# Sinkhorn attention with a mixture of experts: later queries interleaved by ScalarE, keys mixed two rows at a time

## The chip, the core and the metric

One core of a Trainium2 chip. The metric is the device time of one execution in microseconds (us). The first comparison of the kernel before with the changed kernel has four runs of each. A ratio is always the mean of one kernel's fast runs over the mean of the fast runs of before from the same rounds. That is why it is not quite the ratio of the medians that are quoted beside it. A run is "fast" when it lies within 1.5% of the fastest run of the same kernel; all runs that are compared were fast, or "unknown" where there was only one.

## The reference

Block attention: in each of 32 (batch, head) pairs the 768 rows fall into 8 blocks of 96. A Sinkhorn matrix P, from five rounds of row and column normalization, mixes the blocks of keys and values; each block of queries then attends to one mixed block. A mixture of four experts follows.

```python
k_sorted = np.einsum('bhij,bhjcd->bhicd', P, k_b)        # v the same way
scores = scale * np.matmul(q_b, k_sb.transpose(0, 1, 2, 4, 3))   # per block
attn = softmax(scores)
x = matmul(attn, v_sb)            # [4, 8, 768, 64] -> rows of 512
for e in range(4):
    out += p[:, e:e+1] * (np.maximum(x @ w1[e], 0) @ w2[e])
```

## The kernel before

Batch 0's attention is the "head" of the program (to about 45 us). While TensorE works on one batch's experts, the attention of the next batch runs in slots between groups of matmuls, by a fixed plan. In this program the matmuls write their results to PSUM and read their operands from SBUF. `psA` and `psM` are two pools of PSUM with two buffers each; keys, values, scores and averages of the attention share `psA`.

```python
PLAN = [(0, 0, st_q, 0), (0, 1, st_v, 0), ..., (0, 6, st_s, 0), ..., (0, 9, st_a, 0), ...]  # (chunk, slot, stage, pair of heads)

def load_queries(b, heads=range(H)):            # one DMA a head, rows of 64 floats
    ...
    for h in heads:
        nc.gpsimd.dma_start(t[:, h // 2, :, h % 2, :], q[b, h].rearrange("(t p) d -> p t d", p=P))

def st_q(b, pr):                                # queries of two heads, transposed by the DMA
    nc.sync.dma_start_transpose(qT[:], natural[(b, "q")][:, pr].rearrange("p t h d -> p (t h d)"))

def st_k(b, pr):                                # keys: mixed and transposed in one matmul
    for r in range(R):                          # R = 6
        for hh in range(2):
            nc.tensor.matmul(ps[ds(D * hh, D), r, :], head(b, "k", h)[:, r, :], PIk..., ...)
    nc.scalar.copy(kT..., ps...)                # one copy, 128x768

def st_s(b, pr):                                # scores, then the exponential
    for i in range(NB):
        for hh in range(2):
            nc.tensor.matmul(pss[hh]..., kT[...], qT[ds(D * hh, D), i, :], ...)
    for hh in range(2):
        nc.scalar.activation(ETs[...][:, 0:S].rearrange("c (a x) -> c a x", a=2), pss[hh][0:BLK, :, 0:HS], AF.Exp, ...)
```

The softmax here doesn't subtract the row's maximum and nothing guards it: scores larger than these inputs give would overflow.

## Time and profile before

| | before |
|---|---|
| time, median of 4 | 374.87 us (374.79 to 375.55) |
| span of the profiled run | 373.0 us |
| TensorE busy | 366.3 us |
| ScalarE busy | 73.9 us |
| exponential of a score group | 24 x 0.802 us |

TensorE's own waits are the measure here: it is busy nearly all the time, so a change helps only by giving it less to do or by removing an idle stretch, and hurts by making one. The prediction shows these lines.

### The profile page before, as it was taken

To read this page: it belongs to the slowest core of one execution; us is meant where nothing else is said; L and a number is where in the kernel's file an instruction comes from. 1 tells how busy PE (TensorE), PEld (TensorE's weight loads), DVE (VectorE), ACT (ScalarE), POOL (GpSimd) and SP (SyncE) were. 2 spreads that over 40 slices of the span, in tenths; PEclk is the share of its full clock that TensorE was granted. 3 is DMA by queue.
4 is the path that set the end of the run, shared out by engine and by line. 5 is a ranking of instruction groups with operands and counts; after the bars stand their busy time and mean duration, and the time that the engine had idled before them with its cause. 6 is when DMAs were issued, how large, how long until landed. Compare 5 with 4: busy or idle time off the path is not lost.

```text
span 373.0 us, 9188 instructions
## 1 busy us (share of the span) xinstructions
PE 366.3 (98%) x4013; PEld 314.9 (84%) x4013; DVE 261.2 (70%) x470; ACT 73.9 (20%) x120; POOL 87.9 (24%) x122
## 2 busy tenths in 40 slices
PE   8999999999999999999999999999999999999996
PEld 8785858888888888888898888888889888888885
DVE  5654798679888774795694684696695693774872
ACT  2673330423210233012100224012101000000000
POOL 8772101804577203002911000000000001001001
PEclk9999999999999999999999999999999999999999
DMA  7999999999995658642962322505203101121001
GB/s 104 207 207 229 208 209 197 190 163 143 187 154 137 110 77 133 126 80 43 124 71 48 101 66 60 138 2 77 79 2 79 57 15 44 56 47 50 19 3 56
DMA packets 69603, 38.25 MB, mean 103 GB/s; under 512 B 40374, under 2 KB 64444, under 8 KB 69564
## 3 DMA queue, kind: packets, MB, share of 16 engines
q0 software_dynamic: 34640, 17.83, 37.6%
q1 hardware_dynamic: 34924, 19.85, 26.0%
q8 instruction: 31, 0.51, 0.6%
q14 instruction: 8, 0.07, 0.1%
HBM read 42.00 MB, written 6.34 MB: 130 GB/s over the span
## 4 chain that ended last, share of the span: by engine, by line
PE 87%; DMA 8%; DVE 2%; POOL 1%; issue 1%; ACT 0%; DVEq 0%
PE ps_h L730 40%; PE ps_p L763 35%; DMA w<-in_moe_w_dram 4%; PE ps_o L670 3%; DMA qT<-natq 2%; PE ps_w L241 2%; DMA natq<-in_q_dram 2%; PE ps_h L635 1%; PE ps_s L393 1%; PE ps_a L425 1%; PE ps_k L376 1%; PE ps_v L345 1%; POOL sn L284 0%; DVE xsl L410 0%; POOL T L136 0%
## 5 line engine op out<-in xcount | busy, mean ns | idle before, releaser
L730 PE MATMUL ps_h<-xT,w 128*128 128x256 f16 x1440 | 163.0, 273 | 0.0
L730 PEld LDWEIGHTS <-w 128*128 128x128 f16 x1440 | 139.5, 98 | 17.8
L736 DVE SCALAR_TENSOR_TENSOR Hb<-ps_h,pb 128x1024 f16<-128x1024 f32 x90 | 110.1, 1224 | 40.1 <-PE ps_h L730 38.3
L763 PEld LDWEIGHTS <-Sb 128*128 128x128 f16 x720 | 69.5, 98 | 9.6 <-issue 0.5
L763 PEld LDWEIGHTS <-Hb 128*128 128x128 f16 x540 | 52.1, 98 | 6.8 <-issue 0.4
L790 POOL TENSOR_TENSOR oa<-u,p 128x256 f32<-128x256 f32 x9 | 6.5, 723 | 176.7 <-issue 161.9
L763 PE MATMUL ps_p<-w,Sb 128*128 128x256 f16 x360 | 43.2, 273 | 0.3 <-DVE u L863 0.3
L763 PE MATMUL ps_p<-w,Hb 128*128 128x256 f16 x360 | 43.2, 273 | 0.0
L763 PE MATMUL ps_p<-T,Sb 128*128 128x256 f16 x360 | 42.3, 273 | 0.0
L400 ACT ACTIVATE ET<-ps_s 96x768 f16<-96x768 f32 x24 | 18.1, 802 | 54.4 <-PE ps_s L393 54.4
L114 POOL DMA_DIRECT2D natq<-in_q_dram x24 | 19.9, 851 | 14.3 <-DMA w<-in_moe_w_dram 10.2
L778 ACT COPY p<-ps_p 128x256 f32<-128x256 f32 x9 | 3.4, 373 | 93.3 <-PE ps_p L763 50.1
L763 PE MATMUL ps_p<-T,Hb 128*128 128x256 f16 x180 | 21.6, 273 | 0.0
L715 DVE TENSOR_TENSOR Sb<-Sb,Hb 128x512 f16<-128x512 f16 x45 | 19.6, 436 | 0.4
L717 DVE TENSOR_TENSOR Sb<-Hb 128x512 f16<-128x512 f16 x45 | 18.8, 418 | 0.0
L713 DVE TENSOR_TENSOR Sb<-Hb 128x512 f16<-128x512 f16 x45 | 18.8, 417 | 0.0
L410 DVE TENSOR_TENSOR xsl<-ps_a,rz 96x512 f16<-96x512 f32 x24 | 16.5, 686 | 0.8
L719 DVE TENSOR_TENSOR Sb<-Hb,Sb 128x512 f16<-128x512 f16 x45 | 16.6, 427 | 0.0
L383 ACT CAST kT<-ps_k 128x768 f16<-128x768 f32 x12 | 9.6, 799 | 35.4 <-PE ps_k L376 35.3
L788 DVE TENSOR_TENSOR u<-ps_p,p 128x256 f32<-128x256 f32 x9 | 3.8, 426 | 17.9 <-PE ps_p L763 17.9
L351 ACT CAST vo<-ps_v 128x768 f16<-128x768 f32 x12 | 9.5, 801 | 21.5 <-PE ps_v L345 19.8
L103 POOL DMA_DIRECT2D nat_k<-in_k_dram x8 | 6.1, 767 | 31.9 <-PE ps_k L376 27.8
(131 smaller groups left out, 300.9 us busy)
## 6 DMA issues: line engine op xcount, KB each, us to landing
w<-in_moe_w_dram POOLq DMA_DIRECT2D x7, 1024.0 KB, 27.1
pb<-p_dram SPq DMA_DIRECT2D x12, 512.0 KB, 5.1
nat_k<-in_k_dram POOLq DMA_DIRECT2D x8, 384.0 KB, 7.4
nat_v<-in_v_dram POOLq DMA_DIRECT2D x8, 384.0 KB, 8.6
vs<-vo SPq DMA_DIRECT2D x36, 66.0 KB, 4.6
natq<-in_q_dram POOLq DMA_DIRECT2D x24, 96.0 KB, 4.5
out_dram<-ob SPq DMA_DIRECT2D x9, 256.0 KB, 2.3
out_dram<-oa SPq DMA_DIRECT2D x9, 256.0 KB, 2.3
```

The lines of the kernel that those rows point to most:

```text
L114: nc.gpsimd.dma_start(t[:, h // 2, :, h % 2, :], q[b, h].rearrange("(t p) d -> p t d", p=P))
L383: nc.scalar.copy(kT[:, 0:S].rearrange("p (i r c) -> p i r c", i=NB, r=R), ps.rearrange("p r (i c) -> p i r c", c=CP),)
L400: nc.scalar.activation(ETs[2 * (pr % 2) + hh][:, 0:S].rearrange("c (a x) -> c a x", a=2), pss[hh][0:BLK, :, 0:HS], AF.Exp, bias=0.0, scale ...
L410: nc.vector.tensor_tensor(xsl[:, :, hh, :].rearrange("c (a i) d -> c a i d", a=2), av[:, :, :, 0:D], rz[:].broadcast_to([BLK, 2, HB, D]), ...
L670: nc.tensor.matmul(ps, h0(fc)[:, ds(t * P, P)], w2sb[0][:, fc, :], start=(fc == 0), stop=(fc == NFC - 1),)
L713: tt(sm[0], blk(0, 1), blk(1, 1), ALU.add)
L715: tt(sm[1], sm[0], blk(0, 0), ALU.subtract)
L717: tt(sm[2], blk(0, 0), blk(0, 1), ALU.subtract)
L719: tt(sm[3], blk(1, 0), sm[1], ALU.subtract)
L730: nc.tensor.matmul(ps[:, f, :], w1sb[e][:, kc, ds((4 * g + f) * P, P)], xT[:, kc, ds(2 * c * P, 2 * P)], start=(kc == 0), stop=(kc == NKC ...
L736: nc.vector.scalar_tensor_tensor(out=Hb[:, e, ds(4 * g, 4), :], in0=ps[:], scalar=0.0, op0=ALU.max, in1=pb[:, ds(e, 1), :].broadcast_to([P ...
L763: nc.tensor.matmul(ps[:], lhs(e, f), Ts[e][rhs][:, f, :], start=(e == es[0] and f == 0), stop=(e == E - 1 and f == KH - 1),)
```

## The change

The intent: queries are loaded in large contiguous pieces as keys are, which saves many small packets, and keys need half as many matmuls, each at full width. The price is paid on ScalarE, which is idle four fifths of the time: a copy that interleaves the queries, four key copies for one, and an exponential that writes its columns back in the old order.

```diff
 def st_q(b, pr):
-    nc.sync.dma_start_transpose(qT[:], natural[(b, "q")][:, pr].rearrange("p t h d -> p (t h d)"))
+    nc.scalar.copy(qi.rearrange("p (r h d) -> p h r d", r=R, h=2), natural[(b, "q", pr // 2)][:, ds(2 * (pr % 2), 2), :, :])
+    nc.sync.dma_start_transpose(qT[:], qi)
 def st_k(b, pr):
-    ... 12 matmuls of 64 columns of weights; one copy of 128x768
+    for hh in range(2):
+        for a in range(R // 2):
+            nc.tensor.matmul(pk[:, hh, a, :], head(b, "k", h)[:, ds(2 * a, 2), :].rearrange("p r d -> p (r d)"), PIk..., ...)
+    ... four copies of 64x384
 def st_s(b, pr):
-                qT[ds(D * hh, D), i, :],
+                qT[ds(D * hh, D), :, ds(i * CP, CP)],
 ...
-            ETs[...][:, 0:S].rearrange("c (a x) -> c a x", a=2),
-            pss[hh][0:BLK, :, 0:HS],
+            ETs[...][:, 0:S].rearrange("k (a i c r) -> k a i r c", a=2, i=HB, r=R),
+            pss[hh][0:BLK, :, 0:HS].rearrange("k a (i r c) -> k a i r c", i=HB, r=R),
 # head: the query transposes of both halves move behind the fifth exponential; 30 filler matmuls
#       (their results are not used, they keep TensorE busy) for 20 + 12
 # first batch of experts: p1 in psA instead of psM; p6 read out before a weight sum; PLAN0 reordered
 # end: the last output is stored in two halves
```

More of the change, by code (lines that the diff above doesn't have):

```diff
@@ L99, in load_natural @@
     def load_natural(b, nm, qd):
-        src = {"k": k, "v": v}[nm]
+        src = {"q": q, "k": k, "v": v}[nm]
         t = nat.tile([P, 4, R, D], F16, name=f"nat_{nm}_{b}_{qd}", tag=f"nat_{nm}")
@@ L106, in load_natural @@
         )
-    def load_queries(b, heads=range(H)):
-        if (b, "q") not in natural:
-            natural[(b, "q")] = nat.tile([P, NPB, R, 2, D], F16, name=f"natq_{b}", tag="natq", bufs=1)
-        t = natural[(b, "q")]
-        for h in heads:
-            nc.gpsimd.dma_start(t[:, h // 2, :, h % 2, :], q[b, h].rearrange("(t p) d -> p t d", p=P))
     def head(b, nm, h):
@@ L237, in warm @@
     def warm(n):
-        ps = psA.tile([P, 4, P], F32, tag="ps", name=f"ps_w_{state['n']}")
+        ps = psM.tile([P, 4, P], F32, tag="ps", name=f"ps_w_{state['n']}")
         state["n"] += 1
@@ L259 @@
     scol = const.tile([GH, NB, 1], F32, name="scol")
-    sn16 = const.tile([GH, NB, NB, CP], F16, name="sn16")
+    sn16_q = const.tile([P, NB * NB * CP], F16, name="sn16_q")
+    sn16 = sn16_q[0:GH].rearrange("g (i j c) -> g i j c", i=NB, j=NB)
+    qi = sn16_q[:, 0:2 * R * D]
     warm(84)
@@ L265 @@
         nc.scalar.activation(sn[:], sn[:], AF.Exp, bias=0.0, scale=1.0)
-        if it >= 3:
-            h_q(it - 3, 0, nc.scalar.copy)
-            warm(20 - 8 * (it - 3))
+        if it == 4:
+            for qd in range(2):
+                h_q(qd, 0, nc.scalar.copy)
+            warm(30)
         nc.vector.tensor_reduce(srow[:], sn[:], AX.X, ALU.add)
@@ L365, in st_q @@
         qT = att.tile([P, R, P], F16, name=f"qT_{b}_{pr}", tag="qT", bufs=3)
-        nc.sync.dma_start_transpose(
-            qT[:], natural[(b, "q")][:, pr].rearrange("p t h d -> p (t h d)")
-        )
-        qTs[(b, pr)] = qT.rearrange("p t x -> p (t x)").rearrange("p (i x) -> p i x", i=NB)
+        nc.scalar.copy(
+            qi.rearrange("p (r h d) -> p h r d", r=R, h=2),
+            natural[(b, "q", pr // 2)][:, ds(2 * (pr % 2), 2), :, :],
+        )
+        nc.sync.dma_start_transpose(qT[:], qi)
+        qTs[(b, pr)] = qT
     def st_k(b, pr):
-        ps = psa([P, R, P], F32, f"ps_k_{b}_{pr}")
-        for r in range(R):
-            for hh in range(2):
-                h = 2 * pr + hh
+        ps = psa([P, 2, 512], F32, f"ps_k_{b}_{pr}")
+        pk = ps[:, :, 0:R // 2 * P].rearrange("p h (a x) -> p h a x", x=P)
+        for hh in range(2):
+            h = 2 * pr + hh
+            for a in range(R // 2):
                 nc.tensor.matmul(
-                    ps[ds(D * hh, D), r, :],
-                    head(b, "k", h)[:, r, :],
+                    pk[:, hh, a, :],
+                    head(b, "k", h)[:, ds(2 * a, 2), :].rearrange("p r d -> p (r d)"),
                     PIk[(b * H + h) // 4][:, h % 4, :, :].rearrange("p i c -> p (i c)"),
@@ L381, in st_k @@
                 )
-        kT = kTs[pr % 2]
-        nc.scalar.copy(
-            kT[:, 0:S].rearrange("p (i r c) -> p i r c", i=NB, r=R),
-            ps.rearrange("p r (i c) -> p i r c", c=CP),
-        )
+        kT = kTs[pr % 2][:, 0:S].rearrange("p (i a r c) -> p r a i c", a=R // 2, r=2, c=CP)
+        for hh in range(2):
+            for r in range(2):
+                nc.scalar.copy(
+                    kT[ds(D * hh, D), r],
+                    pk[ds(D * r, D), hh].rearrange("p a (i c) -> p a i c", c=CP),
+                )
     def st_s(b, pr):
@@ L400, in st_s @@
             nc.scalar.activation(
-                ETs[2 * (pr % 2) + hh][:, 0:S].rearrange("c (a x) -> c a x", a=2),
-                pss[hh][0:BLK, :, 0:HS],
+                ETs[2 * (pr % 2) + hh][:, 0:S].rearrange("k (a i c r) -> k a i r c", a=2, i=HB, r=R),
+                pss[hh][0:BLK, :, 0:HS].rearrange("k a (i r c) -> k a i r c", i=HB, r=R),
                 AF.Exp, bias=0.0, scale=SCALE,
@@ L566, in h_x, with st_lq @@
         )
-    def st_n(b, pr):
-        load_queries(b, range(2 * pr, 2 * pr + 2))
     def st_lv(b, qd):
         load_natural(b + 1, "v", qd)
-    def st_lq(b, _):
-        load_queries(b + 1)
+    def st_lq(b, qd):
+        load_natural(b + 1, "q", qd)
     def st_lk(b, qd):
@@ L581, in stage @@
         f(b, pr)
-        nm = {st_k: "k", st_v: "v"}.get(f)
+        nm = {st_k: "k", st_v: "v", st_q: "q"}.get(f)
         if nm and pr % 2 and 1 < b < B - 1:
             load_natural(b + 1, nm, pr // 2)
-        if f == st_s and pr == NPB - 1 and 1 < b < B - 1:
-            load_queries(b + 1)
     PLAN = [
@@ L600 @@
     PLAN0 = [
-        (0, 9, st_v, 0), (0, 10, st_q, 0), (0, 10, st_v, 1), (0, 11, st_k, 0), (0, 11, st_n, 1), (1, 0, st_q, 1),
-        (1, 0, st_s, 0), (1, 0, st_n, 2), (1, 1, st_k, 1), (1, 1, st_v, 2), (1, 2, st_v, 3), (1, 3, st_a, 0),
-        (1, 4, st_x, 0), (1, 3, st_q, 2), (1, 4, st_n, 3), (1, 5, st_s, 1), (1, 6, st_k, 2), (1, 8, st_a, 1),
-        (1, 7, st_lv, 0), (1, 9, st_x, 1), (1, 10, st_s, 2), (1, 9, st_lv, 1), (1, 9, st_q, 3), (1, 11, st_k, 3),
-        (1, 12, st_a, 2), (1, 12, st_lk, 0),
-        (2, 0, st_lq, 0), (2, 1, st_x, 2), (2, 2, st_lk, 1), (2, 2, st_s, 3), (2, 8, st_a, 3), (2, 9, st_x, 3),
+        (0, 9, st_v, 0), (0, 10, st_q, 0), (0, 10, st_v, 1), (0, 11, st_k, 0), (1, 0, st_q, 1),
+        (1, 0, st_s, 0), (1, 1, st_k, 1), (1, 1, st_lq, 0), (1, 2, st_k, 2), (1, 3, st_q, 2), (1, 4, st_s, 1),
+        (1, 5, st_v, 2), (1, 6, st_v, 3), (1, 7, st_lv, 0), (1, 7, st_a, 0), (1, 8, st_x, 0), (1, 9, st_a, 1),
+        (1, 9, st_q, 3), (1, 10, st_x, 1), (1, 10, st_lv, 1), (1, 11, st_s, 2), (1, 12, st_lk, 0),
+        (2, 0, st_a, 2), (2, 0, st_lq, 1), (2, 1, st_k, 3), (2, 2, st_x, 2), (2, 2, st_lk, 1), (2, 3, st_s, 3),
+        (2, 8, st_a, 3), (2, 9, st_x, 3),
     ]
@@ L757, in chunk, with product @@
         sm = lambda n: (lambda e, f: Sb[:, n, e, ds(f * P, P)])
-        def product(n, lhs, rhs):
-            ps = psm([P, DH], F32, f"ps_{n}_{b}_{c}")
+        def product(n, lhs, rhs, pool=psm):
+            ps = pool([P, DH], F32, f"ps_{n}_{b}_{c}")
             for e in es:
@@ L783, in chunk @@
             slot()
+            parts = 2 if (b, c) == (B - 1, R // 2 - 1) else 1
+            if parts == 2:
+                nc.sync.dma_start(o[:, 2 * c, 0:DH], oa1)
             nc.scalar.copy(p5[:], product("p5", sm(0), "t1"))
@@ L797, in chunk @@
             slot()
-            nc.sync.dma_start(o[:, 2 * c, :], oa[:])
+            if parts == 2:
+                nc.sync.dma_start(o[:, 2 * c, DH:Dm], oa2)
+            else:
+                nc.sync.dma_start(o[:, 2 * c, :], oa[:])
             return
         def f1():
-            nc.scalar.copy(p1[:], product("p1", blk(0, 0), "b11"))
+            nc.scalar.copy(p1[:], product("p1", blk(0, 0), "b11", psa))
             slot()
@@ L861, in chunk @@
                 h_sums(e, 4)
-            next(sums0)
             tt(u2[:], product("p6", sm(1), "t2"), p1[:], ALU.add)
             slot()
+            next(sums0)
             gtt(oa2, u2[:], oa2, ALU.add)
-            next(sums0)
             tt(u3[:], product("p7", sm(2), "t3"), u2[:], ALU.add)
@@ L869, in chunk @@
             last(u3[:])
+            next(sums0)
             store(1, ob)
@@ L948 @@
     for qd in range(2):
-        for nm in ("v", "k"):
+        for nm in ("v", "k", "q"):
             load_natural(1, nm, qd)
-        if qd == 0:
-            load_queries(1, range(2))
     later = [
@@ L959 @@
         [(h_w, 0, vec), (h_s, 1, 2)],
-        [(h_w, 1, vec), (h_a, 0, 2)],
+        [(h_w, 1, act), (h_a, 0, 2)],
         [(h_s, 0, 3), (h_a, 1, 2)],
```

## The prediction

The 20 warm-up matmuls in it (ps_w, 128x128) have 128 moving columns, as the new key matmuls do.

> **What bounds the kernel now.** I read the page's busy shares first, then the waits, then TensorE's timeline, then the chain of waits.
>
> ```profile
> PE 366.3 (98%) x4013; PEld 314.9 (84%) x4013; DVE 261.2 (70%) x470; ACT 73.9 (20%) x120; POOL 87.9 (24%) x122
> ```
>
> TensorE is busy for 366.3 of 373.0 us, ScalarE for a fifth. So moving work to ScalarE is nearly free if no wait comes of it, and a gain must be less TensorE work or one of the last 6.7 idle microseconds. These are the idle times by releaser (waits of TensorE: total, times, longest):
>
> ```profile
> PE ps_w L241 <- DVE Hb L141: 1.1, 1, 1.1
> PE ps_R L296 <- DVE sn L284: 0.5, 1, 0.5
> PE ps_s L393 <- DMA qT<-natq: 0.3, 1, 0.3
> PE ps_p L763 <- DVE u L863: 0.3, 1, 0.3
> PE ps_a L534 <- DVE xsl L546: 0.2, 1, 0.2
> PE ps_o L670 <- DMA w<-in_moe_w_dram: 0.2, 1, 0.2
> ```
>
> They sum to 2.6 us; the rest is mostly the tail: the last matmul ends near 369.4 us and the span ends at 373.0. Removing every wait would give 0.7%, so 2% (7.5 us) is out of reach of waits alone.
>
> The costs of the mixing, in TensorE's timeline (start, duration, count; the end is modelled, so I take the difference of starts):
>
> ```profile
> 66.27 1.47 PE L763 MATMUL ps_p<-T,Sb 128*128 128x256 f16 x12
> 67.58 0.49 PE L345 MATMUL ps_v<-nat_v,PIv 128*128 128x384 f16 x2
> 67.90 1.47 PE L763 MATMUL ps_p<-T,Sb 128*128 128x256 f16 x12
> ...
> 91.06 1.47 PE L763 MATMUL ps_p<-T,Sb 128*128 128x256 f16 x12
> 92.47 0.51 PE L393 MATMUL ps_s<-qT,kT 64*128 64x96 f16 x16
> 92.91 1.48 PE L763 MATMUL ps_p<-T,Sb 128*128 128x256 f16 x12
> 94.33 0.53 PE L376 MATMUL ps_k<-PIk,nat_k 128*64 128x128 f16 x12
> 94.78 1.48 PE L763 MATMUL ps_p<-w,Sb 128*128 128x256 f16 x12
> 96.11 0.65 PE L425 MATMUL ps_a<-vs,ET 96*128 96x65 f16 x16
> ```
>
> A group of 12 product matmuls takes 1.31 us when the next group has the same shape (66.27 to 67.58), but 1.41 or 1.42 when a group of halves follows (91.06 to 92.47; 92.91 to 94.33). So a key group costs 94.78 - 94.33 = 0.45 us plus about 0.10 us in front of it. A value group of the same 768 moving columns, at full width, costs 67.90 - 67.58 = 0.32 us and nothing in front.
>
> [...] the 20 warm-up matmuls of that shape start at 9.18 us, the next group at 10.40, 61 ns each. [...] the trace has 802 for the exponential and 799 for the key copy; [...] the head's 128x384 casts take 0.48 us. [...] The queries are read in rows of 64 floats, 256 B; 24 x 768 = 18,432 of the page's 40,374 packets under 512 B are these. Their 96 KB took 6.8 and 8.5 us (median) to land in the busy windows 66 to 73 and 73 to 78 us.
>
> **The change part by part.**
>
> *Keys, two rows at a time.* 12 half-width matmuls per pair become 6 full ones of 128 columns. At 53 ns (a third of the value matmul's 160) to 61 ns (warm-up) they cost 0.32 to 0.37 us; I take 0.36[...]. Saved: 0.45 + 0.10 - 0.36 = 0.19 to 0.20 us a pair; 12 pairs give **2.4 us**, all on TensorE, the bound. This is the core of the gain.
>
> *What the keys cost ScalarE.* One copy of 799 ns becomes four of 64x384, about 480 ns each: 1.9 us, 1.1 more per pair, 13 us in all. The score groups follow at least two slots (3.5 us) later in the steady plan, so this should stay hidden.
>
> *Queries.* Per pair, ScalarE copies 128x768 f16 (0.80 us, as the head's copy of that size), 12 pairs, 9.6 us; ScalarE goes from 73.9 to about 97 us, 26%. The query loads become six of contiguous rows instead of 24 of short ones: POOL saves 19.9 - 6 x 0.77 = 15 us of issuing, not on the path; the DMA between 68 and 80 us gets lighter.
>
> *Scores.* The moving operand is now 6 pieces of 16 columns. The head already reads its queries so: 205 ns a matmul there against 203 here; no cost. The exponential writes with a step of 6 elements; no row shows that form. Doubled it would still fit: 24 x 0.8 us more on an engine idle for 275 us.
>
> *Removed waits.* The 0.3 before the second pair's scores (7.9 us from issue to landing of qT, itself waiting for a query load that took 7.0 in the chain) should go with the small packets. The 0.3 on u L863 goes, because p6 is now read out before the 1.2 us weight sum; but the last scores' xT is issued at 114.1 and lands about 3.2 us later, near 117.3, while the next layer would want it at 117.6: I count **0.2**. The key matmul and the wait together, from the second pair on: 11 x 0.2 + 0.3 + 0.2 = 2.7 us.
>
> *Tail.* The last output goes in two halves, the first stored earlier; the last transfer is 128 instead of 256 KB, of the 2.1 us to landing. I count **0.4**.
>
> *Head.* ScalarE's copy of queries at 9.29 to 10.09 us held up the fifth Sinkhorn step: exponentials come at 4.12, 5.92, 7.67, then at 9.98 rather than about 9.43. Moving it gives 0.55 us there, and handing a copy from VectorE to ScalarE the 0.2 of xsl. But the DMA runs at about 208 GB/s without a break from 8 to 66 us, and w2 of the first expert lands at 28.46, just after TensorE asks for it. So I expect the 0.55 to reappear as a longer wait there: **0** by the time of 70 us.
>
> **A new wait** I expect. These are the queues of SyncE (issue times):
>
> ```profile
> 65.74 1.31 SPq L366 DMA_TRANSPOSE qT<-natq  x1
> 68.97 3.90 SPq L359 DMA_DIRECT2D vs<-vo  x6
> ```
>
> The first qT is issued at 65.74, as soon as two heads of queries land, and takes 6.8 us: 72.5, with the scores at 72.93. Only 0.4 us to spare. After the change four heads have to land: the load behind the keys (28.89 + 35.4 = 64.3) needs the 1.9 us that keys took behind values (62.4), so 66.2. Then ScalarE is in the value copy (66.47 to 67.27), copies the queries until about 68.0, and only then comes the transpose: 68.0 plus 5.5 to 6.8 us is 73.5 to 74.8. The scores are asked for at about 72.6. Everything gained before that point goes into this wait, and compared with 72.93 the pair starts 0.6 to 1.9 us later; I take **+1.3**.
>
> **Sum.** +1.3 (first scores, all earlier gains swallowed) - 2.7 - 0.4 = -1.8, or 373.0. If the load is quicker than I think, the first scores come where they did or 0.3 earlier: 371.4. I weigh the two about 60 to 40: **372.4 us**, 0.6% faster.
>
> **The rivals.**
> 1. *The query path does not hold.* The transpose lands in time; every gain before 70 us counts if w2 also comes earlier: -2.4 - 0.3 - 0.2 - 0.4 - 0.2 - up to 0.5, about 370.8. For it: fewer packets. Against: the 0.4 us of slack and two new steps in series.
> 2. *The query path holds worse.* A single interleave buffer makes each copy wait for the transpose before it[...]; the second and third pairs follow within four slots in batch 1. Two waits of 2 us would give 375. Against: later batches have at least three slots (5 us) between such copies.
> 3. *ScalarE's latency takes the place.* A strided exponential that is much slower, with four key copies, delays the two PSUM buffers that scores, keys and values share; 0.3 us for 12 pairs would be 3.6 us and undo the keys: 375. Against: ScalarE is 20% busy and the slots are 1.75 us wide.
> 4. *Full-width keys are worth less*: [...] 374.
>
> **Range and chances.** Rival 1 sets the low end, a little lower for a better tail; rivals 2 to 4, partly together, the high end: 370.6 to 374.3. Neither 367.3 nor 382.3 is near: faster 0.02, same 0.96, slower 0.02.
>
> **What would show it.** Right: key groups of 6 start 0.32 to 0.37 us before the next group, and the group before them takes 1.31; ScalarE near 97 us; the waits of 0.3 on qT (second pair) and u gone; one new wait at the first ps_s of batch 1, on the DMA of qT, of 1 to 2 us; w2's wait at 28 us grown to about 0.7; the span's end 0.4 us closer to the last matmul. Wrong: no wait at the first scores (then 371 or below), waits of ps_s on ScalarE's kT, of ps_k or ps_v on the exponential, an exponential well over 0.8 us[...].

## The result, and the profile after

The changed kernel takes 389.38 us (387.76 to 391.51, 4 runs) against 374.87: ratio 1.0386, 95% interval 1.0335 to 1.0438. It is slower by nearly 4%. The busy shares and TensorE's waits of the changed kernel (total, times, longest):

```profile
PE 368.0 (95%) x3939; PEld 317.7 (82%) x3939; DVE 260.1 (67%) x469; ACT 141.6 (37%) x169; POOL 71.4 (18%) x104
```

```profile
PE ps_a L428 <- ACT ET L402: 5.1, 3, 2.0
PE ps_p L761 <- ACT ET L402: 2.1, 1, 2.1
PE ps_k L376 <- ACT ET L402: 1.9, 2, 1.5
PE ps_R L292 <- DVE sn_q L280: 1.9, 1, 1.9
PE ps_s L395 <- DMA qT<-sn_q: 1.2, 1, 1.2
...
PE ps_v L341 <- ACT ET L402: 1.0, 1, 1.0
```

ScalarE was expected near 97 us and stands at 141.6. Four of these lines name the exponential (ET), seven waits of 10.1 us together; before there was none. The group of the exponential, before and then after (the mean in ns follows the busy time):

```profile
L400 ACT ACTIVATE ET<-ps_s 96x768 f16<-96x768 f32 x24 | 18.1, 802 | 54.4 <-PE ps_s L393 54.4
```

```profile
L402 ACT ACTIVATE ET<-ps_s 96x768 f16<-96x768 f32 x24 | 63.9, 2852 | 35.3 <-PE ps_s L395 35.3
```

The same number of elements takes 3.6 times as long. How that reaches TensorE is seen in the timeline of the changed kernel's ScalarE, then TensorE (start, duration, what; in brackets the idle time before and its releaser):

```profile
76.88 5.31 ACT L402 ACTIVATE ET<-ps_s 96x768 f16<-96x768 f32 x2
81.82 4.14 ACT L385 CAST kT<-ps_k 64x384 f16<-64x384 f32 x8
85.98 0.83 ACT L362 COPY sn_q<-nat_q 128x768 f16<-128x768 f16 x1
86.84 5.31 ACT L402 ACTIVATE ET<-ps_s 96x768 f16<-96x768 f32 x2
```

```profile
79.67 0.49 PE L376 MATMUL ps_k<-PIk,nat_k 128*128 128x128 f16 x6 [1.51 <-ACT ET L402]
...
82.33 0.49 PE L376 MATMUL ps_k<-PIk,nat_k 128*128 128x128 f16 x6 [0.42 <-ACT ET L402]
...
89.63 0.48 PE L341 MATMUL ps_v<-nat_v,PIv 128*128 128x384 f16 x2 [1.01 <-ACT ET L402]
```

The scores of a pair fill both buffers of psA, and each is free only when its exponential has read it: 2.85 us and 5.31 us after they begin, where it was 0.8 and 1.5. The next keys or values want a buffer one or two slots (1.3 to 1.75 us each) later. ScalarE then works without a break from 76 to 92 us, so later copies queue up behind: the keys mixed from 79.67 us on are copied from 81.82 on, after the pair of exponentials that started at 76.88.

Where the 14.7 us between the two spans went, by the start of the same matmuls in both (in brackets: what this stretch adds):

| reached at (us) | before | after |
|---|---|---|
| first scores of batch 1 | 72.93 | 75.79 (+2.86) |
| first expert layer of batch 1 | 117.92 | 130.24 (+9.46) |
| first expert layer of batch 3 (no attention after it) | 290.68 | 305.77 (+2.77) |
| last sum (VectorE) | 369.39 | 384.48 (0.00) |
| end of the span | 373.0 | 387.7 (-0.4) |

The first row is reached before the first slow exponential: it is the new head and the new wait on qT. In the second row the five waits on the exponential are 7.0 us. To these comes the clock granted to TensorE: after the waits that end at 92.20 and 109.05 us it was 0.50 for about three microseconds (93 to 96 and 110 to 113 us), where it was 1.00 in the kernel before. From the clock of each stretch between 92 and 115 us (0.61 for 92 to 95, 0.96 for 95 to 107, 0.59 for 109 to 113) I estimate a loss of 3.4 us. The faster keys and two small waits that went take back 1.3 us (3 x 0.22 + 0.31 + 0.32). In the third row two waits of 1.55 us on the exponential and two of 0.4 us on the value copies behind it are 3.9 us, of which the faster keys (eight pairs) take back 1.8; about 0.7 us is not assigned.

### The profile page after: what moved, and what is told of

The parts are those of the page before. It is cut to its first block, busy times and chain, and to the rows that moved or that the text cites. A ratio compares the mean times of both kernels' runs of the same rounds, so it can differ in the third digit from the quotient of the medians.

```text
span 387.7 us, 9056 instructions
## 1 busy us (share of the span) xinstructions
PE 368.0 (95%) x3939; PEld 317.7 (82%) x3939; DVE 260.1 (67%) x469; ACT 141.6 (37%) x169; POOL 71.4 (18%) x104
## 2 busy tenths in 40 slices
DMA packets 54099, 38.25 MB, mean 99 GB/s; under 512 B 21670, under 2 KB 49068, under 8 KB 54060
## 4 chain that ended last, share of the span: by engine, by line
PE 83%; ACT 8%; DMA 5%; issue 2%; POOL 1%; DVE 1%; ACTq 0%; DVEq 0%; POOLq 0%
PE ps_h L728 38%; PE ps_p L761 32%; ACT ET L402 6%; DMA nat_v<-in_v_dram 3%; PE ps_h L633 3%; PE ps_o L668 3%; DMA qT<-sn_q 1%; PE ps_a L428 1%; PE ps_s L395 1%; PE ps_v L341 1%; ACT kT L385 1%; PE ps_k L376 1%; PE ps_s L520 1%; PE ps_mv L465 0%; PE ps_a L537 0%
## 5 line engine op out<-in xcount | busy, mean ns | idle before, releaser
L728 PE MATMUL ps_h<-xT,w 128*128 128x256 f16 x1440 | 164.7, 274 | 0.0
L402 ACT ACTIVATE ET<-ps_s 96x768 f16<-96x768 f32 x24 | 63.9, 2852 | 35.3 <-PE ps_s L395 35.3
L761 PEld LDWEIGHTS <-Hb 128*128 128x128 f16 x540 | 53.0, 99 | 9.4 <-issue 2.6
L385 ACT CAST kT<-ps_k 64x384 f16<-64x384 f32 x48 | 22.9, 477 | 26.8 <-PE ps_k L376 26.1
L428 PE MATMUL ps_a<-vs,ET 96*128 96x65 f16 x192 | 8.6, 193 | 5.9 <-ACT ET L402 5.1
L428 PEld LDWEIGHTS <-ET 96*128 96x128 f16 x192 | 7.7, 97 | 6.8 <-ACT ET L402 5.5
```

The lines of the kernel that those rows point to most:

```text
L385: nc.scalar.copy(kT[ds(D * hh, D), r], pk[ds(D * r, D), hh].rearrange("p a (i c) -> p a i c", c=CP),)
L402: nc.scalar.activation(ETs[2 * (pr % 2) + hh][:, 0:S].rearrange("k (a i c r) -> k a i r c", a=2, i=HB, r=R), pss[hh][0:BLK, :, 0:HS].rearr ...
L428: nc.tensor.matmul(ps[:, i // HB, ds((i % HB) * VW, D + 1)], ET[:, ds(i * BLK, P)], vs[:, i, 2 * (pr % 2) + hh, 0:D + 1], start=True, stop ...
L728: nc.tensor.matmul(ps[:, f, :], w1sb[e][:, kc, ds((4 * g + f) * P, P)], xT[:, kc, ds(2 * c * P, 2 * P)], start=(kc == 0), stop=(kc == NKC ...
L761: nc.tensor.matmul(ps[:], lhs(e, f), Ts[e][rhs][:, f, :], start=(e == es[0] and f == 0), stop=(e == E - 1 and f == KH - 1),)
```

## The experiments

**First group: is it the exponential's writing, and can it be had otherwise?**

`e1_exp_reads_step`: same reorder, but the step moves from the output to the input in PSUM.

```diff
-            ETs[...][:, 0:S].rearrange("k (a i c r) -> k a i r c", ...), pss[hh][0:BLK, :, 0:HS].rearrange("k a (i r c) -> k a i r c", ...)
+            for at in range(2):
+                ETs[...][:, ds(at * HS, HS)].rearrange("k (i c r) -> k i c r", ...), pss[hh][0:BLK, at, 0:HS].rearrange("k (i r c) -> k i c r", ...)
```

> The changed kernel, but the score exponential goes through its elements in the order in which it writes them: writes contiguous, reads from PSUM with a step of 16 elements (two instructions of 384 columns for one of 768). Theory (writing with a step of six f16 elements is what makes the exponential 2.85 us): each of the 384-column instructions takes about 0.5 us, TensorE's waits on the exponential (10.1 us in the changed kernel's trace) go, and the time falls to 373.5 to 376.5 us. Rival 1 (a step costs on either side): 1.4 us per instruction, time stays at 387 to 391. Rival 2 (the waits came from the other additions to ScalarE, four key copies and the query copy): the instruction is quick but over 4 us of waits on ScalarE stay, 379 or more.

Measured: 374.03 us (373.5 to 375.34, 4 runs), before 376.46 in the same rounds, ratio 0.9932 (0.9869 to 0.9994). The exponential's group, and the waits:

```profile
L403 ACT ACTIVATE ET<-ps_s 96x384 f16<-96x384 f32 x48 | 19.5, 486 | 38.3 <-PE ps_s L395 38.2
```

```profile
PE ps_s L395 <- DMA qT<-sn_q: 2.6, 1, 2.6
```

No wait on the exponential is left. Four key copies and the query copy are still there, so they were not the cause; both rivals fall. By the same matmuls as in the table, e1 takes 43.36 us from the first scores of batch 1 to its first expert layer (76.44 to 119.80), the changed kernel 54.45, and e1 takes 4.6 us less from there to batch 3: 15.7 us for the form of the exponential alone.

`e2_order_by_matmul`: the plain exponential; the score matmul reads its queries in the old order.

```diff
-                qT[ds(D * hh, D), :, ds(i * CP, CP)],
+                qT[ds(D * hh, D), :, ds(i * CP, CP)].rearrange("p r c -> p c r"),
```

> The changed kernel, but the order is restored one step earlier: the score matmuls read their moving queries in the old column order (step of 128 elements between neighbours), and the exponential is the plain one of the kernel before. Theory (the step costs ScalarE, not TensorE): exponential back at 0.80 us, score groups of 16 still 0.45 us, time 373 to 376 us. Rival (TensorE's moving read also pays for the step): score groups well over 0.45 us; at twice the time 12 x 0.45 = 5.4 us more, 378 to 382.

Measured: 386.58 us (385.82 to 388.32), ratio 1.0268 (1.0212 to 1.0324). The score matmuls:

```profile
L395 PE MATMUL ps_s<-qT,kT 64*128 64x96 f16 x192 | 17.7, 336 | 3.0 <-DMA qT<-sn_q 3.0
```

In e1 the same group is 6.2 us at 204 ns. The rival holds, and more strongly than put: a moving operand whose neighbours lie 128 elements apart cost 11.5 us of TensorE's time here, while pieces of 16 neighbours (e1 and the changed kernel, 204 ns) cost no more than the kernel before (204 ns).

`e3_keys_alone`: the kernel before with the new `st_k` alone.

> The kernel before with the new key mixing alone (6 full matmuls, four key copies). Theory: key groups 0.33 us[...], 0.22 us less per pair, 12 pairs: 2.6 us, 372.2 us. Rival (the four copies delay the scores or the PSUM buffers): waits on kT or on the copies, 373.5 us or more.

Measured: 373.8 us (373.19 to 377.03), ratio 0.994 (0.9876 to 1.0004), so by the times alone not settled. In its trace the stretch from 118.89 to 289.83 us (the same two expert layers as in the table) takes 170.94 us instead of 172.76: 1.82 us for eight pairs, 0.23 a pair, as the theory has it. Before that the rival has a part as well: two waits of 0.7 us on qT and one of 0.6 us on kT.

`e4_probe`: forms of ScalarE writing measured by themselves, in the last batch, where ScalarE is idle.

> The kernel before with nine ScalarE instructions over 96x768 f16 in SBUF, in the last batch, where ScalarE is idle: exponential plain (twice), writing with a step of 2, writing with a step of 6, reading with a step of 16 and writing contiguous, step of 6 with f32 output, a copy with a step of 6, and a copy of 384 f32 with a step of 3. Theory (write step is the cost, whatever the function): plain about 0.82 us, both f16 step-6 writes about 2.85 us, the read step about 0.82; what step 2 and 4-byte elements do is open. Rival (an effect of the exponential or of PSUM as source): step-6 from SBUF 0.82, or the copy quick and the exponential slow.

The steps of six, read from SBUF, took 2.79 us (exponential) and 2.81 us (copy), so it is neither the function nor PSUM. The copy of 384 four-byte elements with a step of three took 0.72 us. The other forms were merged in the profile; e8 below repeats them.

**Second group: the slow exponential alone, the forms apart, and what e1 still waits for.**

`e7_slow_exp_alone`: the kernel before, with the output pattern of the changed kernel and nothing else.

> The kernel before with the changed kernel's way of writing the exponential alone (step of six elements); its result is wrong on purpose, as queries stand in the other order. Theory: 2.85 us per exponential, TensorE waits on it at scores to averages two or three slots apart and at PSUM buffers, 6 to 12 us longer, 381 to 388. Rival (ScalarE is idle enough in the kernel before, and only the three additions together make it late): under 3 us longer.

Measured: 389.09 us (387.35 to 389.78), before 375.80, ratio 1.0335 (1.0287 to 1.0382): 13.3 us by the medians, even more than the theory's range. The exponential is at 2854 ns, and TensorE waits on it; these are the three largest groups of waits:

```profile
PE ps_a L425 <- ACT ET L400: 3.7, 3, 1.6
PE ps_k L376 <- ACT ET L400: 3.6, 3, 1.5
PE ps_v L345 <- ACT ET L400: 2.0, 1, 2.0
```

So the one pattern, without any of the other additions, makes the loss; and e1, with all the other additions and without the pattern, has none of it. The result counted as correct although queries stood in another order. That is no contradiction: worked out from the reference, rows of one block of attention output differ from their mean by 0.4% of their size (scores of these inputs are tiny), so the comparison can't see the order of rows within a block. The order in e1 and later rests on reading the pattern: it writes the same place from the same source as the changed kernel.

`e8_probe_by_line`: 

> The probe again, each form on a line of its own. From the merged one: plain 0.84 us, step-6 write 2.79, copy with step 6 2.81, f32 with step 6 1.59. Open: step-2 f16 write and the step-16 read, one near 1.07 us, the other near 1.4. Theory: the read is the cheaper; plain f32 output is 0.84 us.

ScalarE's timeline of the probe. In order: two plain exponentials, f16 written with a step of 2, of 6, f16 read with a step of 16, f32 written with a step of 6, f32 written plain, a copy with a step of 6, a plain copy.

```profile
285.81 0.84 ACT L992 ACTIVATE ET<-ET 96x768 f16<-96x768 f16 x1
286.69 0.84 ACT L993 ACTIVATE ET<-ET 96x768 f16<-96x768 f16 x1
287.56 1.07 ACT L994 ACTIVATE ET<-ET 96x768 f16<-96x768 f16 x1
288.67 2.79 ACT L995 ACTIVATE ET<-ET 96x768 f16<-96x768 f16 x1
291.50 1.59 ACT L996 ACTIVATE ET<-ET 96x768 f16<-96x768 f16 x1
292.99 1.59 ACT L997 ACTIVATE vo<-ET 96x768 f32<-96x768 f16 x1
294.60 0.84 ACT L998 ACTIVATE vo<-ET 96x768 f32<-96x768 f16 x1
295.35 2.76 ACT L999 COPY ET<-ET 96x768 f16<-96x768 f16 x1
298.15 0.83 ACT L1000 COPY ET<-ET 96x768 f16<-96x768 f16 x1
```

In these forms the cost goes with the step (two elements 1.07 us, six 2.79) and with the width of the element (f32 with a step of six 1.59), not with the function (the copy with a step of six 2.76). The read from SBUF is not free as e4 expected, nor cheaper than the step-2 write as e8 did: 1.59 us against 1.07. Only the read from PSUM in e1 cost nothing extra (486 ns for 384, against 477 for the casts of 384).

`e5_queries_first`: e1, with the first queries loaded ahead of values and keys, and their copy and transpose two slots earlier.

```diff
-        for nm in ("v", "k", "q"):
+        for nm in ("q", "v", "k"):
             load_natural(1, nm, qd)
-   (0, 9, st_v, 0), (0, 10, st_q, 0),
+   (0, 8, st_q, 0), (0, 9, st_v, 0),
```

> e1_exp_reads_step with the queries of batch 1 loaded ahead of its values and keys and interleaved two slots earlier. Theory (the 2.6 us wait at the first scores of batch 1 comes from the queries landing behind values and keys, then passing ScalarE and the transpose in series): the wait falls below 0.5 us, about 2 us less than e1, 0.985 to 0.99 of the kernel before. Rival (the transpose is slow by itself there, or the values now come late): a wait of over 1.5 us stays at the first scores or turns up at the first values.

Measured: 372.74 us (372.4 to 374.44, 6 runs), before 375.80, ratio 0.9919 (0.9887 to 0.995). A wait of 1.7 us stays: the transpose starts at 63.90 us instead of 69.08, but then takes 10.4 us instead of 7.2 from issue to landing. The rival has the larger part.

`e6_old_head`: e1 with the head of the kernel before. 

> e1_exp_reads_step with the head of the kernel before (query transposes one quarter at a time in the last two Sinkhorn steps, warm-up in their place). Theory (the new head leaves TensorE idle before ps_R and its clock falls in 12 to 20 us): the granted clock stays at 1.00 there, the first group of ps_o begins 0.5 to 1.3 us earlier than in e1; but the first scores wait for the DMA of qT anyway, so the time is within 0.5 us of e1 and the wait on qT grows by what the head gained. Rival (the head counts in full): 1 us less than e1.

Measured: 374.92 us (373.68 to 375.6), ratio 0.9966 (0.9935 to 0.9997); e1's interval overlaps it. The first ps_o starts at 28.67 instead of 29.71, and the wait on qT grows from 2.6 to 3.0: whatever the head gains or loses is largely taken up by that wait. After that wait the clock was lower (0.93 over 66 to 90 us, 1.00 in e1; the 16 ps_h matmuls from 76.52 us on took 2.81 us, 1.76 in e1), which took the gain back: the next keys start at 79.33, against 78.65 in e1. A difference in time between the heads is not shown.

**Third and fourth group: can the wait on the first transpose be removed?**

`e9_loads_deferred` is e5 with the second halves of queries and values loaded when the first keys are mixed. `e10_deferred_old_head` is the same with the old head.

> e5_queries_first with the second halves of batch 1's queries and values loaded only after the first keys are mixed (four loads instead of six in flight while the first transpose runs). Theory (the 10.4 us of the first transpose in e5 is the DMA's share among those loads, which last until 77 us): the transpose lands within 8 us of its issue near 64, the wait at the first scores goes (under 0.3 us), 1.4 to 1.7 us less than e5: ratio 0.984 to 0.989. Rival (the transpose is slow there whatever else runs): a wait of over 1 us stays. A cost could be a late second half: a wait at the third pair's queries or values.

> e9_loads_deferred with the head of the kernel before. If the new head is worth its 0.55 us once nothing later swallows it, this is 0.3 to 0.8 us slower than e9; if the first expert's w2 pins the head (first group of ps_o at the same time in both), the two are within 0.3 us; if the new head's idle stretch costs clock, this one is faster.

Measured: 374.87 us (373.67 to 376.43), ratio 0.9961 (0.9927 to 0.9995), and 375.18 us (372.37 to 376.73), ratio 0.9968 (0.9929 to 1.0006). The first transpose, issue to landing, in e5 and then in e9:

```profile
qT<-sn_q SPq DMA_TRANSPOSE x1, 10.4
```

```profile
qT<-sn_q SPq DMA_TRANSPOSE x1, 5.4
```

The two are not issued at the same time: e9's profiled run was the slowest of its six, with a clock of 0.50 from 16 to 24 us, and its transpose is issued at 66.64 us, e5's at 63.90. The cleaner comparison is e10, with the same loads as e9 and the transpose issued at 63.31: 7.6 us, below the 8 of the theory. So the theory of the shared DMA holds for this transpose by some 2.8 us, and the wait at the first scores is gone in both. But it comes back at the second pair, whose transpose now runs beside the deferred loads and takes 8.4 us in e9 and 9.2 in e10, against 5.2 in e5: a wait of 2.0 us in e9, 2.8 in e10. The load was moved, not removed. The two heads again can't be told apart.

`e11_longer_warm` is e5 with 60 filler matmuls for 30; `e12_five_loads` is e5 with only the second values deferred and the next batch's queries four slots later.

> e5_queries_first with 60 instead of 30 filler matmuls ahead of ps_R. Theory (where the first 84 filler matmuls run quickly, TensorE is idle 1.5 to 1.9 us before ps_R, and in some executions the granted clock then halves until 24 us, which costs up to 2 us): the idle time before ps_R falls below 0.3 us, the clock of 12 to 24 us is 1.00 in every profile, and the times are as quick as e5's quick ones, with less spread: 372 to 373. Rival (30 more fillers delay the head by as much as they take, 0.3 to 1.3 us, where the fillers run slowly): 373 to 374.

> e5_queries_first with the second half of the values loaded at the start of the second chunk, and the next batch's queries four slots later, so that five loads instead of six stand behind the first transpose and fewer beside the second. Theory (the transposes share the DMA with the loads; e9 moved the wait from the first to the second pair by moving two loads beside the second): both waits together under 1.2 us, against 1.7 in e5, 0.5 us or more less than e5. Rival (any load moved is paid by the next transpose): 1.7 us or more of waits on qT in all.

e11: 374.6 us (373.07 to 375.65), before 375.67, ratio 0.9955 (0.9917 to 0.9994). The idle time before ps_R is gone and the clock stays at 1.00, but the first values of batch 1 start at 67.62 us, later than in e5 (65.84): the rival. e12: 372.4 us (371.7 to 376.21), ratio 0.9915 (0.9865 to 0.9966); waits on qT of 1.6 and 0.4 us, not under 1.2 as hoped. Its first scores still start 10.6 us after the transpose that they wait for is issued (63.63 to 74.23; 10.5 in e5), so moving one load out of six gave nothing there. Against e5's ratio of 0.9919 no gain is shown. Both e5 and e12 beat the kernel before by some 0.8%, less than the 2% that counts as faster, and the changed kernel by far more.

## Why the prediction was wrong, point by point

**The failed step** is the sentence on scores: "The exponential writes with a step of 6 elements; no row shows that form. Doubled it would still fit: 24 x 0.8 us more on an engine idle for 275 us." It was 2.85 us, not 0.8 or 1.6, and it did not fit: idle time of ScalarE as a share says nothing of how long two PSUM buffers stay taken. With 1.5 us for two exponentials the next user of a buffer comes after they are done, with 5.31 us it comes before. Rival 3 named this mechanism and its mark, but it put 0.3 us on a pair, against "ScalarE is 20% busy and the slots are 1.75 us wide"; and the top of the range, 374.3, lay below the 375 that rivals 2 and 3 themselves gave. e7 (13.3 us from this alone) and e1 (none without it) settle it.

Nor had I measured the form by itself before I built the sum on it. The probe e8 does so with one instruction for each form: 2794 ns with the step of six, 843 plain. Why the write is slow is not shown.

**Keys: right, slightly small.** The groups of six take 0.33 us (71.05 to 71.38), and the products before them 1.31 (69.74 to 71.05), with nothing added in front. With 0.45 + 0.10 before, that is 0.22 a pair; the stretch of eight pairs in e3 gives 0.23, where 0.20 was predicted. Rival 4 falls: 0.33 us for six is 55 ns each. TensorE's lines of the changed kernel:

```profile
69.74 1.47 PE L761 MATMUL ps_p<-T,Sb 128*128 128x256 f16 x12
71.05 0.50 PE L376 MATMUL ps_k<-PIk,nat_k 128*128 128x128 f16 x6
71.38 1.47 PE L761 MATMUL ps_p<-T,Hb 128*128 128x256 f16 x12
```

**Score matmuls: right.** 0.45 us a group and 204 ns a matmul with pieces of 16 columns, 204 ns before.

**Other additions to ScalarE: right.** Key copies 477 ns (480 predicted), query copy 863 ns (800), and without the slow exponential ScalarE is at 98.9 us in e1 (97 predicted). They cost TensorE nothing there.

**The new wait at the first scores: right.** Predicted 1 to 2 us, caused by a query load, a copy and a transpose in series; 1.2 us in the changed kernel, where the transpose took 5.8 us, and 2.6 in e1, where it took 7.2 (5.5 to 6.8 predicted). Its reason was incomplete: e5 and e10, which issue it at nearly the same time, show that the transpose's own time depends on the loads beside it, 10.4 against 7.6 us.

**The head: half right.** The fifth exponential came at 9.44 us (9.43 predicted), 0.54 earlier. But the fillers did not stretch to the new end of the Sinkhorn steps: TensorE sat idle for 1.87 us before ps_R in the changed kernel's profile and the granted clock fell, which I had not foreseen. Two stretches before, then after (columns: stretch, its length, busy time and count of TensorE, weight loads, VectorE, ScalarE, GpSimd, then the granted clock, DMA share and GB/s):

```profile
12.00:16.00 4.00, 3.49 (x108) 3.01 (x108) 2.65 (x7) 1.78 (x4) 3.86 (x5) 1.00 1.26 207
16.00:20.00 4.00, 3.89 (x87) 3.32 (x83) 2.58 (x7) 3.92 (x8) 4.00 (x7) 1.00 1.12 207
```

```profile
12.00:16.00 4.00, 3.48 (x96) 2.91 (x94) 2.24 (x6) 1.65 (x3) 3.49 (x5) 0.77 1.26 207
16.00:20.00 4.00, 3.56 (x66) 3.02 (x62) 1.35 (x4) 2.57 (x5) 3.11 (x7) 0.50 1.14 208
```

The first ps_o starts 2.0 us later (30.48 against 28.46), and the longer wait on w2 that I had named as a sign (0.7 us) did not come: TensorE gets there only at 30.48 and waits for nothing. What decides the clock stays open: with the new head the clock fell in the profiles of the changed kernel, e1 and e9 (0.50, 0.61 and 0.50 for 16 to 20 us), but not in those of e2, e5 and e12 (1.00), where TensorE idled for 1.4 to 1.5 us, while e1 idled only 0.57. The first 84 fillers themselves took 6.2 to 7.7 us from run to run.

**Waits on u and on the second pair's qT: right where they can be seen.** In e1, e5 and the changed kernel neither is among TensorE's waits; in e9, e10 and e12, with other loads beside the transpose, and in e11, with e5's loads, the second wait is back (0.4 to 2.8 us).

**The tail: right.** From the last sum's start to the end 3.2 us instead of 3.6, as predicted.

**Parts I had not counted.** In batch 0 the product p1 moved to psA, the pool of the attention. In the changed kernel it waits 2.1 us for the exponential to free a buffer, and the clock in the three microseconds after it (92 to 95 us) is 0.61. I had counted every wait at its length, but after some waits the clock was lower too. After waits of 2.96 us (e2), 2.97 (e6), 2.77 (e10) and 2.03 (e7, just after one of 1.03) the next 16 ps_h matmuls took 2.8 to 3.1 us instead of 1.76, and the clock of 66 to 90 us is 0.93; after 2.01 us (the changed kernel at 109.05) the clock is 0.50 for 110 to 113 us. After 2.61 us (e1) and 2.05 (e9, e11) it is 1.00 for 66 to 90 us, so the length of one wait does not decide it; what does is not shown.

## What to carry to other kernels

A reorder that an instruction does "on the way" is priced by its access pattern: put the step on the side that was cheap when measured, here ScalarE's read from PSUM (486 ns for 384 elements, 477 for the plain casts of 384), and not on a 2-byte write to SBUF (2.85 us for 0.80) or a matmul's moving operand (336 ns for 204). Before calling work on an idle engine free, ask for how long it holds the buffers that the bound engine needs next (here 5.31 us instead of 1.5 for a pair); the engine's busy share (37%) doesn't tell. The clock can be lower after a wait of the bound engine (0.50 for about three microseconds after waits of 2.1 and 2.0 us in the changed kernel, but 1.00 after one of 2.61 in e1), so look at the clock after it. And where a form of instruction has no row in the profile, measure it by itself before a sum is built on it.

## What was measured of these forms

- ScalarE, 96x768 elements, plain: 843 ns for the exponential and 832 for the copy from SBUF to SBUF (e8), 802 for the exponential from PSUM (before).
- ScalarE writing to SBUF with a step (e8): f16 with a step of two elements 1073 ns, with a step of six 2794 (exponential) and 2762 (copy); f32 with a step of six 1587. So the step in bytes alone does not order the forms: 24 bytes (f32) took less than 12 bytes (f16).
- ScalarE reading with a step: f16 from SBUF with a step of 16 elements 1587 ns for 768 (e8); f32 from PSUM with a step of 16 elements 486 ns for 384 (e1), against 477 for the contiguous reads of the key copies.
- A matmul's moving operand, 96 columns, neighbours 256 bytes apart: the score groups rose from 6.2 to 17.7 us for 192 matmuls (e2).
- The DMA transpose of the first queries beside loads: 5.4 us (e9) to 10.4 us (e5) from issue to landing. In e11 the scores that wait for it start 11.7 us after its issue (64.75 to 76.49).
